# Attention and MoE kernel: the rest of q and k loaded two tokens to a partition, even tokens ahead of odd ones, and turned by halves of the partitions

## The chip, the cores and the metric

The kernel runs on one core of a Trainium2 chip. The metric is the device time of one execution in microseconds (us), where lower is better. Fast executions of one kernel agree within 1.5%. Medians below are of all executions, and ratios of the fast ones alone.

A core has five engines with queues of their own: TensorE (matmuls, "PE" in the profile, with "PEld" for its weight loads), VectorE ("DVE"), ScalarE ("ACT"), GpSimd ("POOL") and SyncE ("SP"). SyncE computes nothing here: it issues DMAs, which 16 DMA engines then carry out.

## The reference

```python
# q, k, v: (8, 8, 576, 64) float32, f: (8, 8, 576); w_in (512, 2048), w_out (2048, 512)
scores = q @ k^T / 8
cum = cumsum(log(clip(f, 1e-4, 1)), axis=-1)
scores = where(causal, scores + cum[..., :, None] - cum[..., None, :], -1e9)
attn = softmax(scores) @ v                      # "forgetting" attention
x = attn.transpose(0, 2, 1, 3).reshape(4608, 512)
h = x @ w_in
out = (h * sigmoid(h)) @ w_out
```

## The kernel before

A sequence of 576 tokens is handled as a first block of 128, then a **rest** of three blocks of 128 and a tail of 64. A **unit** is one batch and a pair of heads; there are 32. For each unit the rest of q and k passes through four steps. SyncE loads it in float32, GpSimd casts it to bf16, SyncE issues a DMA transpose (a **turn**) that puts the head dimension on the partitions, and TensorE computes scores. Between these, TensorE works off matmuls of the MoE part, the **filler work**, in an order fixed at build time.

```python
    def load_qk(n):                                   # 4 DMAs a unit, runs of 256 bytes
        b, p = divmod(n, NP)
        ts = []
        for name, src in (("qf", q), ("kf", k)):
            t = stage.tile([P, NR, 2, D], FP32, name=name, tag=name, bufs=4)
            for i in range(2):
                nc.sync.dma_start(
                    out=t[:, :, i, :],
                    in_=src[b, head(p, i), P:SM, :].rearrange("(c p) d -> p c d", p=P),
                )
            ts.append(t)
        qst[n] = tuple(ts)
    ...
    def transposes(n):                                # one turn a unit
        src = qbf.pop(n)
        t = qktp.tile([P, NX, P], BF16, name="qkT", tag="qkT")
        qkT[n] = t[:, :, :].rearrange("p x c -> p (x c)")
        nc.sync.dma_start_transpose(
            out=t[:, :, :], in_=src[:, :, :].rearrange("p x c -> p (x c)")
        )
    ...
    def prepare(n):                                   # loads run 4 units ahead, turns 2
        ...
        if n > 1 and n + 4 < NU:
            load_qk(n + 4)
        if 0 < n < NU - 2:
            cast_qk(n + 2)
            transposes(n + 2)
```

SyncE also loads v (four DMAs a batch) and the tails, and from the fifth pair of units on it turns the attention output x. All of that stands in one queue, in order.

The softmax here doesn't subtract the row's maximum and nothing guards it: scores larger than these inputs give would overflow.

## Time and profile before

| | before |
|---|---|
| time, median of 4 | 349.33 us (347.66 to 349.63) |
| profiled span, mean granted TensorE clock | 346.0 us, 0.995 |
| TensorE busy | 332.3 us (96%) |
| SyncE, from the gate behind the weights to the end of the last turn | 222.4 us: 228 issues of 199.9 us in sum, gaps 22.5 us |
| score matmuls of units 16 to 28 | one unit every 7.17 us |

The gate is a small DMA at 36 us that makes SyncE wait for half of w_out. An issue is the time that SyncE spends on one DMA instruction, not the transfer.

### The profile page before, as it was taken

Reading aid. Unit: us, or ns where it says so; the run is one execution under the profiler, and the core shown is the slowest. Engines: PE = TensorE matmul, PEld = TensorE weight load, DVE = VectorE, ACT = ScalarE, POOL = GpSimd, SP = SyncE. Lnnn points to the kernel's source line nnn. Section 1 sums busy time; section 2 is a strip of 40 time slices with the busy share of each in tenths; the row PEclk is TensorE's granted clock in tenths of the full one; section 3 lists DMA queues with packets and bytes.
Section 4 is the critical chain, followed back from the end, with each engine's and each line's share of the span. In section 5 each row is a group of like instructions: output and inputs, shape, how many; then the busy total and the mean of one; then the engine's idle time right before and its main releaser. Section 6 shows DMA issues by size and latency. Waiting matters only on the chain.

```text
span 346.0 us, 8849 instructions
## 1 busy us (share of the span) xinstructions
PE 332.3 (96%) x3521; PEld 199.3 (58%) x3567; DVE 180.2 (52%) x389; ACT 216.7 (63%) x401; POOL 128.5 (37%) x227
## 2 busy tenths in 40 slices
PE   7899999998899999999999999999999999999995
PEld 3645656576466566566565666656656565555654
DVE  4655835457267566445545545555655454344330
ACT  5757735777657857758658686585776844454431
POOL 8886316732637082163155028208320000001011
PEclk9989999999999999999999999999999999999999
DMA  8999999999999999997697979989733010001012
GB/s 153 177 189 220 184 182 163 241 211 200 174 189 214 192 197 159 167 223 164 137 213 139 170 168 184 172 171 208 139 83 66 11 61 34 30 31 63 30 50 73
DMA packets 141497, 50.44 MB, mean 146 GB/s; under 512 B 132368, under 2 KB 138768, under 8 KB 141456
## 3 DMA queue, kind: packets, MB, share of 16 engines
q1 hardware_dynamic: 131440, 32.70, 54.7%
q0 software_dynamic: 9856, 17.04, 21.7%
q8 instruction: 28, 0.46, 0.6%
q10 hardware_dynamic: 160, 0.13, 0.2%
q14 instruction: 13, 0.11, 0.1%
HBM read 36.85 MB, written 9.44 MB: 134 GB/s over the span
## 4 chain that ended last, share of the span: by engine, by line
PE 73%; DMA 16%; POOL 4%; issue 3%; SPq 3%; ACT 0%; POOLq 0%
PE po L612 31%; PE hp L567 28%; PE sc L459 6%; DMA vf<-in_v_dram 5%; PE dn L506 4%; DMA w_out_bf<-in_moe_w_out_dram 3%; DMA qktf<-in_k_dram 3%; PE dn L515 2%; DMA w_in_bf<-in_moe_w_in_dram 2%; DMA qkT<-qkb 2%; SPq L158 2%; DMA qkb<-in_k_dram 1%; POOL vp L413 1%; DMA kf<-in_k_dram 1%; SPq L168 1%
## 5 line engine op out<-in xcount | busy, mean ns | idle before, releaser
L576 DVE SCALAR_TENSOR_TENSOR gt<-th,hp 128x384 bf16<-128x384 bf16 (+2 forms) x208 | 105.5, 521 | 84.7 <-ACT th L575 81.3
L575 ACT ACTIVATE th<-hp 128x384 bf16<-128x384 f32 (+2 forms) x208 | 95.2, 479 | 86.3 <-PE hp L567 84.2
L612 PE MATMUL po<-w_out_bf,gt 128*128 128x512 bf16 (+1 forms) x551 | 139.1, 374 | 3.5 <-issue 2.1
L567 PE MATMUL hp<-x,w_in_bf 128*128 128x384 bf16 (+2 forms) x700 | 129.5, 323 | 1.2 <-DVE xt L554 0.7
L567 PEld LDWEIGHTS <-w_in_bf 128*128 128x128 bf16 x832 | 80.1, 98 | 57.6 <-issue 2.6
L591 POOL DMA_DIRECT2D out_dram<-osb x38 | 20.9, 553 | 169.9 <-ACT osb L622 122.6
L463 ACT ACTIVATE u<-sc 128x1024 bf16<-128x1024 f32 (+1 forms) x96 | 75.2, 822 | 10.9 <-PE sc L459 10.9
L612 PEld LDWEIGHTS <-gt 128*128 128x128 bf16 x592 | 53.2, 98 | 48.6 <-issue 3.2
L413 POOL TENSOR_TENSOR vp<-vf,w_bf 128x520 bf16<-128x520 f32 (+1 forms) x32 | 34.5, 1083 | 14.9 <-DMA vf<-in_v_dram 9.4
L622 ACT ACTIVATE osb<-po 128x512 f32<-128x512 f32 (+1 forms) x37 | 22.1, 596 | 18.9 <-PE po L612 18.9
L468 DVE TENSOR_TENSOR u<-u,tri 128x768 bf16<-128x768 bf16 x32 | 22.1, 689 | 21.8 <-ACT u L463 21.8
L459 PE MATMUL sc<-qkT 64*128 64x128 bf16 (+1 forms) x640 | 26.7, 207 | 1.7 <-DMA qkT<-qkb 1.6
L459 PEld LDWEIGHTS <-qkT 64*128 64x128 bf16 x640 | 18.3, 94 | 13.1 <-issue 9.5
L482 DVE TENSOR_TENSOR ut<-ut,trit 128x128 bf16<-128x128 bf16 x32 | 8.2, 257 | 32.6 <-ACT ut L475 32.6
L475 ACT ACTIVATE ut<-sc 128x640 bf16<-128x640 f32 x32 | 23.3, 729 | 0.0
L399 POOL CAST qkb<-qf 128x384 bf16<-128x384 f32 x32 | 16.7, 523 | 16.2 <-PE tp L285 11.8
L506 PEld LDWEIGHTS <-u 128*128 128x128 bf16 x576 | 20.8, 97 | 2.5
L506 PE MATMUL dn<-vp,u 128*128 128x65 bf16 x384 | 21.8, 193 | 0.0
L524 DVE TENSOR_TENSOR xr<-dn,rec 128x448 bf16<-128x448 f32 x32 | 20.0, 624 | 1.1
L506 PE MATMUL dn<-v,u 128*128 128x65 bf16 x192 | 19.8, 193 | 0.0
L567 PE MATMUL hp<-xt,w_in_bf 128*128 128x256 bf16 x128 | 17.7, 273 | 0.0
L399 POOL CAST qkb<-kf 128x384 bf16<-128x384 f32 x32 | 16.9, 527 | 1.0 <-DMA kf<-in_k_dram 1.0
(68 smaller groups left out, 203.9 us busy)
## 6 DMA issues: line engine op xcount, KB each, us to landing
out_dram<-osb POOLq DMA_DIRECT2D x32, 256.0 KB, 3.1
vf<-in_v_dram SPq DMA_DIRECT2D x26, 256.0 KB, 4.7
qf<-in_q_dram SPq DMA_DIRECT2D x64, 96.0 KB, 3.4
kf<-in_k_dram SPq DMA_DIRECT2D x64, 96.0 KB, 3.3
w_in_bf<-in_moe_w_in_dram POOLq DMA_DIRECT2D x4, 512.0 KB, 7.6
w_out_bf<-in_moe_w_out_dram POOLq DMA_DIRECT2D x4, 512.0 KB, 8.7
vf<-in_v_dram POOLq DMA_DIRECT2D x6, 256.0 KB, 9.8
qkb<-in_q_dram POOLq DMA_DIRECT2D x8, 128.0 KB, 5.4
```

Of the source, the lines that this page charges most:

```text
L399: nc.gpsimd.tensor_copy(out=t2[:, c0 : c0 + NR, :].rearrange("p c x -> p (c x)"), in_=t[:, :, :, :].rearrange("p c h d -> p (c h d)"),)
L413: nc.gpsimd.tensor_tensor(out=vbf[b][r, c, :, :], in0=vst[b][c][r, :, :], in1=w_bf[r, c + 1, b * H : (b + 1) * H, None].to_broadcast([n, H ...
L459: nc.tensor.matmul(sc[:, i, o : o + q1 - q0], lhsT=kt, rhs=t[r, q0:q1], start=True, stop=True)
L463: nc.scalar.activation(out=u[:, :, c * SM : c * SM + w], in_=sc[:, :, 0:w], func=ACT.Exp, scale=scale)
L468: nc.vector.tensor_tensor(out=x, in0=x, in1=tri[:, None, None, :].to_broadcast([P, 2, NR, P]), op=ALU.mult,)
L475: nc.scalar.activation(out=ut[:, :, 0:3:2, :].rearrange("p k i t -> p i k t"), in_=sc[:, :, T0 : T0 + (NM + 1) * ST].rearrange("p i (k t) ...
L506: nc.tensor.matmul(dn[:, i * NR + c - 1, :], lhsT=u[:, i, o : o + P], rhs=vals(kb, i), start=(kb == 0), stop=(kb == c),)
L567: nc.tensor.matmul(hp[:, :], lhsT=w_in_bf[:, cc, fc * P : (fc + 1) * P], rhs=xcols(g, cc), start=(cc == 0), stop=(cc == NCC - 1),)
L575: nc.scalar.activation(out=th[:, :], in_=hp[:, :], func=ACT.Tanh, scale=0.5)
L576: nc.vector.scalar_tensor_tensor(out=gt[:, fc, :], in0=th[:, :], scalar=1.0, in1=hp[:, :], op0=ALU.add, op1=ALU.mult,)
L612: nc.tensor.matmul(po[:, :], lhsT=gt[:, fc, tb * P : (tb + 1) * P], rhs=w_out_bf[:, fc, m0:m1], start=(fc == 0), stop=(fc == NFC - 1),)
L622: nc.scalar.activation(out=osb[:, :], in_=po[:, :], func=ACT.Copy, scale=0.5)
```

## The change

The intent is to lighten the DMA engines. Two neighbouring tokens of one head are 512 contiguous bytes in HBM (the chip's main memory), so a partition that takes both gets one run of 512 bytes in place of two of 256. A block of 128 tokens then fills 64 partitions. The two halves of the partitions hold different blocks, so each half is turned by itself. Tokens of a block now stand even ones first, and v, the masks, the decay weights and the output rows follow that order.

```diff
     def load_qk(n):
-        for name, src in (("qf", q), ("kf", k)):
-            t = stage.tile([P, NR, 2, D], FP32, name=name, tag=name, bufs=4)
-            for i in range(2):
+        t = stage.tile([P, NR, 2, 2 * D], FP32, name="qkf", tag="qkf", bufs=4)
+        for j in range(NR):
+            for half in range(2):
+                i, c = HALVES[half][j]
                 nc.sync.dma_start(
-                    out=t[:, :, i, :],
-                    in_=src[b, head(p, i), P:SM, :].rearrange("(c p) d -> p c d", p=P),
+                    out=t[half * HP : (half + 1) * HP, j, :, :],
+                    in_=(q, k)[i][b, h0 : h0 + 3 : 2, P + c * P : 2 * P + c * P, :].rearrange(
+                        "h (p s) d -> p h (s d)", s=2
+                    ),
                 )
...
     def load_v(b, c):
+            for s in range(2):
+                nc.sync.dma_start(
+                    out=t[s * HP : (s + 1) * HP, :, 0:D],
+                    in_=src.rearrange("h (p s) d -> s p h d", s=2)[s],
+                )
...
     def transposes(n):
-        nc.sync.dma_start_transpose(
-            out=t[:, :, :], in_=src[:, :, :].rearrange("p x c -> p (x c)")
-        )
+        for i in range(2):
+            half = 1 - i
+            nc.sync.dma_start_transpose(
+                out=t[:, i, :].rearrange("p (x c) -> p x c", c=HP),
+                in_=src[half * HP : (half + 1) * HP, :, :].rearrange("p x c -> p (x c)"),
+            )
...
-        fill(0.2, 1, (1, 0))
         if m > 0:
             back(m - 1)
...
-        slot(piece - 0.2)
+        slot(piece, 1, 0)
```

Cut from the diff are the table `HALVES` (which block goes to which half), `h0`, the old lines of `load_v` and its tail case, the casts, the new mask, the reordered exponentials of the decay, the column offsets of the score matmuls, and the output rows stored in two parts.

More of the change, by code (lines that the diff above doesn't have):

```diff
@@ L49 @@
     NRUN = P // RUN
+    HP = P // 2
     assert D == 64 and S == 576 and DM == H * D and NP == NCC and B == 8
@@ L78 @@
     trit = const.tile([P, ST], BF16, name="trit")
+    tri2 = const.tile([P, P], BF16, name="tri2")
     ban = const.tile([P, NP, P], BF16, name="ban")
@@ L114, in rows_of @@
         if g < 3:
-            b = tb if g == 0 else 4 + 2 * (g - 1) + tb
-            return [(slice(0, P), b, 0)]
+            t0 = (tb if g == 0 else 4 + 2 * (g - 1) + tb) * S
+            return [(slice(0, P), out[t0 : t0 + P, :])]
         for b in range(B):
             if REST_OF[b] == g:
-                return [(slice(0, P), b, P + tb * P)]
+                t0 = b * S + P + tb * P
+                rows = out[t0 : t0 + P, :].rearrange("(p s) m -> s p m", s=2)
+                return [(slice(s * HP, (s + 1) * HP), rows[s]) for s in range(2)]
         b0 = (0 if g == 3 + NM else NM) + 2 * tb
-        return [(slice(0, ST), b0, SM), (slice(ST, P), b0 + 1, SM)]
+        t0s = [(b0 + i) * S + SM for i in range(2)]
+        return [(slice(i * ST, (i + 1) * ST), out[t0 : t0 + ST, :]) for i, t0 in enumerate(t0s)]
     qk0: dict[int, bass.AP] = {}
@@ L141, in load_v0 @@
         vf0[b] = t
-    qst: dict[int, tuple] = {}
+    qst: dict[int, bass.AP] = {}
     tst: dict[int, bass.AP] = {}
@@ L150, in head @@
         return p // 2 * 4 + 2 * i + p % 2
+    HALVES = ([(0, 0), (0, 2), (1, 0)], [(1, 1), (1, 2), (0, 1)])
     def load_qk(n):
         b, p = divmod(n, NP)
-        ts = []
-        for name, src in (("qf", q), ("kf", k)):
-            t = stage.tile([P, NR, 2, D], FP32, name=name, tag=name, bufs=4)
-            for i in range(2):
+        t = stage.tile([P, NR, 2, 2 * D], FP32, name="qkf", tag="qkf", bufs=4)
+        h0 = head(p, 0)
+        for j in range(NR):
+            for half in range(2):
+                i, c = HALVES[half][j]
                 nc.sync.dma_start(
-                    out=t[:, :, i, :],
-                    in_=src[b, head(p, i), P:SM, :].rearrange("(c p) d -> p c d", p=P),
-                )
-            ts.append(t)
-        qst[n] = tuple(ts)
+                    out=t[half * HP : (half + 1) * HP, j, :, :],
+                    in_=(q, k)[i][b, h0 : h0 + 3 : 2, P + c * P : 2 * P + c * P, :].rearrange(
+                        "h (p s) d -> p h (s d)", s=2
+                    ),
+                )
+        qst[n] = t
     def load_tails(b):
@@ L177, in load_v @@
         t = vfs[c]
-        r = slice(0, P) if c < NR else slice(ST, P)
-        nc.sync.dma_start(
-            out=t[r, :, 0:D],
-            in_=v[b, :, P + c * P : min(S, P + (c + 1) * P), :].rearrange("h p d -> p h d"),
-        )
+        src = v[b, :, P + c * P : min(S, P + (c + 1) * P), :]
+        if c < NR:
+            for s in range(2):
[3 more added lines that the diff above has]
+                )
+        else:
+            nc.sync.dma_start(out=t[ST:P, :, 0:D], in_=src.rearrange("h p d -> p h d"))
         vst[b].append(t)
@@ L253, in weights_scan @@
         nc.vector.tensor_scalar_mul(out=half[:, :], in0=cum[:, S - 1 : S], scalar1=0.5)
-        nc.scalar.activation(
-            out=wexp[:, 0:S], in_=cum[:, :], func=ACT.Exp, bias=half[:, 0:1], scale=-1.0
-        )
+        for r in (slice(0, P), slice(SM, S)):
+            nc.scalar.activation(
+                out=wexp[:, r], in_=cum[:, r], func=ACT.Exp, bias=half[:, 0:1], scale=-1.0
+            )
         nc.vector.tensor_scalar(
@@ L264, in weights_scan, with weights_rest @@
         )
+    def weights_rest():
+        nc.scalar.activation(
+            out=wexp[:, P:SM].rearrange("b (c s p) -> b c p s", s=2, p=HP),
+            in_=cum[:, P:SM].rearrange("b (c p s) -> b c p s", s=2, p=HP),
+            func=ACT.Exp,
+            bias=half[:, 0:1],
+            scale=-1.0,
+        )
+        nc.vector.tensor_copy(out=wexp[:, S : S + ST], in_=wexp[:, SM:S])
     def weights():
@@ L396, in cast_qk @@
         t2 = conv.tile([P, NX, 2 * D], BF16, name="qkb", tag="qkb")
-        for i, t in enumerate(qst.pop(n)):
-            c0 = i * (NR + 1)
-            nc.gpsimd.tensor_copy(
-                out=t2[:, c0 : c0 + NR, :].rearrange("p c x -> p (c x)"),
-                in_=t[:, :, :, :].rearrange("p c h d -> p (c h d)"),
-            )
+        t = qst.pop(n)
+        for x0, j0, j1 in ((0, 0, 2), (5, 2, 3)):
+            for j in range(j0, j1):
+                nc.gpsimd.tensor_copy(
+                    out=t2[:, x0 + 2 * j - 2 * j0 : x0 + 2 * j - 2 * j0 + 2, :].rearrange(
+                        "p s (h d) -> p s h d", h=2
+                    ),
+                    in_=t[:, j, :, :].rearrange("p h (s d) -> p s h d", s=2),
+                )
         nc.gpsimd.tensor_copy(
-            out=t2[:, NR, :].rearrange("s (i d) -> s i d", i=2),
+            out=t2[:, 4, :].rearrange("s (i d) -> s i d", i=2),
             in_=tst[b].rearrange("s (u i w) d -> s u w i d", u=2, w=2)[:, p // 2, p % 2, :, :],
@@ L424, in transposes @@
         src = qbf.pop(n)
-        t = qktp.tile([P, NX, P], BF16, name="qkT", tag="qkT")
-        qkT[n] = t[:, :, :].rearrange("p x c -> p (x c)")
-        nc.sync.dma_start_transpose(
-            out=t[:, :, :], in_=src[:, :, :].rearrange("p x c -> p (x c)")
-        )
+        t = qktp.tile([P, 2, NX * HP], BF16, name="qkT", tag="qkT")
+        qkT[n] = t[:, :, :].rearrange("p i c -> p (i c)")
+        for i in range(2):
[3 more added lines that the diff above has]
+                in_=src[half * HP : (half + 1) * HP, :, :].rearrange("p x c -> p (x c)"),
+            )
+    Q0 = NX * HP
+    QAT = {1: Q0, 2: Q0 - P, 3: Q0 + P, NM: Q0 + 2 * P}
+    KAT = {1: Q0 + 2 * P + HP, 2: 0, 3: P, NM: P + HP}
     T0 = P
     CHUNKS = [
-        [(1, 0, P, 0), (2, P, 2 * P, P), (3, 2 * P, RB, 2 * P), (1, P, 2 * P, RB)],
-        [(0, 0, RB, 0), (1, 2 * P, RB, RB)],
-        [(2, 2 * P, RB, 0)] + [(kb, RB, RQ, T0 + kb * ST) for kb in range(NM + 1)],
+        [(1, QAT[1], P, 0), (2, QAT[2], P, P), (3, QAT[3], P, 2 * P), (1, QAT[2], P, RB)],
+        [(0, QAT[2], RB, 0), (1, QAT[3], P, RB)],
+        [(2, QAT[3], P, 0)] + [(kb, QAT[NM], ST, T0 + kb * ST) for kb in range(NM + 1)],
     ]
@@ L440 @@
     AT = {(c, c): (c - 1) * P for c in range(1, NM)}
-    AT |= {(c, 0): SM + (c - 1) * P for c in range(1, NM)}
+    AT |= {(2, 0): SM, (1, 0): SM + P, (3, 0): SM + 2 * P}
     AT |= {(2, 1): RB, (3, 1): SM + RB, (3, 2): 2 * SM}
@@ L450, in scores @@
         sc = psc.tile([P, 2, SM], FP32, name="sc", tag="sc")
-        for kb, q0, q1, o in CHUNKS[c]:
+        for kb, q0, nq, o in CHUNKS[c]:
             for i in range(2):
                 r = slice(i * D, (i + 1) * D)
-                if kb == 0:
-                    kt = kT0[b][r, p, :]
-                else:
-                    k0 = RB if kb == NM else kb * P + RB
-                    kt = t[r, k0 : k0 + P]
+                kt = kT0[b][r, p, :] if kb == 0 else t[r, KAT[kb] : KAT[kb] + P]
                 nc.tensor.matmul(
-                    sc[:, i, o : o + q1 - q0], lhsT=kt, rhs=t[r, q0:q1], start=True, stop=True
+                    sc[:, i, o : o + nq], lhsT=kt, rhs=t[r, q0 : q0 + nq], start=True, stop=True
                 )
@@ L470, in scores @@
                 in0=x,
-                in1=tri[:, None, None, :].to_broadcast([P, 2, NR, P]),
+                in1=tri2[:, None, None, :].to_broadcast([P, 2, NR, P]),
                 op=ALU.mult,
@@ L589, in store @@
         n = max(n, 0)
-        for q_, dst, src in stores[:n]:
+        for q_, dst, src in sum(stores[:n], []):
             q_.dma_start(out=dst, in_=src)
@@ L622, in m2_part @@
             nc.scalar.activation(out=osb[:, :], in_=po[:, :], func=ACT.Copy, scale=0.5)
-            for n, (r, b, s0) in enumerate(rows_of(g, tb)):
-                t0 = b * S + s0
+            parts = []
+            for n, (r, rows) in enumerate(rows_of(g, tb)):
                 q_ = nc.gpsimd if not last else (nc.scalar if n == 1 else nc.sync)
-                stores.append((q_, out[t0 : t0 + r.stop - r.start, m0:m1], osb[r, :]))
+                parts.append((q_, rows[:, m0:m1], osb[r, :]))
+            stores.append(parts)
     M1 = [(g, fc) for g in range(NG) for fc in range(NFC)]
@@ L729 @@
     turn0(0, 1)
-    nc.vector.tensor_copy(out=wexp[:, S : S + ST], in_=wexp[:, SM:S])
+    weights_rest()
     bans = [ban0(0), ban0(1)]
@@ L782 @@
     load_v0(7)
+    for i in range(2):
+        for j in range(2):
+            make_upper_triangular(
+                nc, tri2[i * HP : (i + 1) * HP, j * HP : (j + 1) * HP], val=1.0, diag=(i <= j)
+            )
     after(w_out_bf[0:1, 2 * NFC // WQ - 1, DM - 16 : DM])
```

## The prediction

> **What bounds the kernel now.** I read the page first (engine shares, DMA queues), then busy time by stretches, the chain of waits in order of time, and last SyncE's own timeline, because the change touches little but what SyncE issues.
>
> ```profile
> PE 332.3 (96%) x3521; PEld 199.3 (58%) x3567; DVE 180.2 (52%) x389; ACT 216.7 (63%) x401; POOL 128.5 (37%) x227
> ...
> DMA  8999999999999999997697979989733010001012
> ...
> q1 hardware_dynamic: 131440, 32.70, 54.7%
> ```
> TensorE is busy for 96% of 346.0 us. The 16 DMA engines are also near full, but only to slice 28 or so (242 us). Queue q1 is SyncE's: 131440 packets of mostly 256 B.
>
> ```profile
> 40.00:90.00 50.00, 46.58 (x563) 30.35 (x569) 27.20 (x62) 31.43 (x63) 23.41 (x38) 1.00 1.07 197
> 90.00:120.00 30.00, 29.68 (x352) 17.83 (x355) 17.40 (x38) 21.33 (x39) 12.24 (x21) 1.00 1.06 193
> 120.00:240.00 120.00, 118.69 (x1378) 71.97 (x1393) 65.12 (x144) 82.18 (x154) 47.83 (x85) 1.00 0.96 177
> 280.00:346.00 66.00, 61.91 (x364) 35.67 (x368) 23.93 (x48) 26.70 (x57) 5.93 (x11) 1.00 0.13 45
> ```
> By stretches (length, TensorE busy, ..., granted clock, DMA share, GB/s): DMA runs at 1.0 from 40 to 240 us, yet TensorE idles only 3.4 us in 40 to 90 and 1.6 us in the next 150. The chain tells the same:
>
> ```profile
> 85.24 3.53 DMA qkT<-qkb
> 88.82 0.40 PE sc L459 x8
> 89.21 0.97 PE po L612 x4
> 90.18 0.44 PE hp L567 x4
> ```
> Up to 88.8 us the chain that ended last runs through loads and turns (DMA transposes) of q and k; after it, through TensorE alone. Four 512-column matmuls take 0.86 to 0.97 us there, some 0.22 to 0.24 us each, and a TensorE that waits for nothing can't be sped up by lighter DMA. All that a perfect load path could win is the idle 3.4 us of 40 to 90: 1% of the span.
>
> The resource that I think decides the case is SyncE's queue:
>
> ```profile
> 129.50 1.10 SPq L158 DMA_DIRECT2D qf<-in_q_dram  x2
> 130.65 1.02 SPq L158 DMA_DIRECT2D kf<-in_k_dram  x2
> 131.78 1.23 SPq L427 DMA_TRANSPOSE qkT<-qkb  x1
> 133.05 2.12 SPq L158 DMA_DIRECT2D qf<-in_q_dram  x2
> 135.22 1.02 SPq L158 DMA_DIRECT2D kf<-in_k_dram  x2
> 136.35 1.22 SPq L427 DMA_TRANSPOSE qkT<-qkb  x1
> 137.61 0.63 SPq L168 DMA_DIRECT2D qktf<-in_q_dram  x1
> 138.28 0.63 SPq L168 DMA_DIRECT2D qktf<-in_k_dram  x1
> 139.01 1.27 SPq L538 DMA_TRANSPOSE x<-xr  x1
> 140.33 1.23 SPq L542 DMA_TRANSPOSE xt<-xr  x1
> ```
> It issues one DMA after another with gaps of some 0.05 us. Summed from this timeline, its issues fill 203 of the 225 us between 37 and 262 us (90%).
>
> ```profile
> L427 SPq DMA_TRANSPOSE qkT<-qkb x32: 1220/1370/2697, 53.4 to 257.9; - x32
> L158 SPq DMA_DIRECT2D kf<-in_k_dram x64: 486/487/1766, 38.0 to 246.0; - x64
> L179 SPq DMA_DIRECT2D vf<-in_v_dram x32: 521/627/2807, 54.9 to 233.9; - x32
> L538 SPq DMA_TRANSPOSE x<-xr x11: 1212/1235/2253, 126.9 to 266.0; - x11
> ```
> These are least, median and longest ns of one issue. The least does not follow the bytes: a turn of seven 128x128 blocks and one of six cost 1.22 and 1.21 us (the one-block xt turn 1.22), and a load some 0.5 us whatever its size.
>
> **What the Trainium skill says.** "Perfetto Trace Analysis", section "DMA Instruction — HWDGE": the profiled window of such an instruction is the locking and use of the descriptor generator, not data movement. Its section "What 'DMA-bound' means" lists, beside the DMA engines, the DMA sequencer, seen as solid DMA slices on the issuing engine's track. The trace agrees: SyncE is 90% solid. "DMA: Bandwidth & Descriptors", section "Specifications", puts the least transfer for line rate at 512 B. In the packet records a 256 B packet takes 18 ns (median; mean 23 under load) and a 4096 B one some 160, so the time does not scale down with size: this is what the change goes for. The same page, "Rules for kernel authors", advises against two transfers to disjoint partition halves in place of one of 128 partitions, since they serialize; the change makes such halves of q/k, v and the turns. No transfer before the change is such a pair, so the trace can't say yet.
>
> **The change part by part.** "Unit" is a head pair of a batch; there are 32, at some 7.1 us of TensorE each in the steady part (score matmuls begin every 14.2 us per pair of units; about 5 us a unit before 90 us).
>
> *Packets, removed.* A unit's q/k rest is 1536 packets of 256 B, then 768 of 512 B. Going by 18 ns and 160 ns, a 512 B packet should take 18 + 256 x 142/3840 = 27 to 28 ns (estimate), so a pair saves 36 - 27.5 = 8.5 ns. These packets are 38% of a unit's 4032 (1536 q/k, 896 v, 256 tails, 896 turn, 448 x turns), so DMA load falls by about a tenth, 0.96 to 0.87. Worth nothing after 90 us, as TensorE does not wait; up to some 2 us of the 3.4 us before.
>
> *SyncE issues, added.* Loads: 4 to 6 a unit, 192 for 128, so +64 at 0.55 us with the gap = +35 us. v: three of four tiles loaded in halves, +24 at 0.67 us (64-partition issues took 0.62 us) = +16 us. Turns: 64 half turns for 32 whole ones. If the 1.22 us is per instruction, +32 x 1.27 = +41 us. If it goes by partitions, 0.61 each, +0. A mixture of base and size, 0.87 each, gives +15 us. Sum: +51, +66 or +92 us.
>
> *SyncE time that can take it.* 22 us of gaps, plus the part of today's issues above their floors. Floors are 127 x 0.49 + 32 x 1.23 + 32 x 0.58 + 20 x 1.23 + 16 x 0.62 = 155 us of the 203, so 48 us is pushback from full DMA engines. It should mostly go with smaller, lighter transfers, but not all, as the weights still stream at 40 us. So 50 to 70 us is free against 51 to 92 us added.
>
> *By the unit.* New floor in the stretch with x turns: loads 6 x 0.56 = 3.35, v 1.75 x 0.67 = 1.17, tails 0.34, x turns 1.27, together 6.1 us, plus half turns 1.3 to 2.55: **7.4 to 8.7 us against 7.1 us of TensorE.** A whole turn now lands some 11 us before its scores (issued at 111.6 and landing in about 4, for scores at 126.7), so a deficit shows only once it has eaten that: at 1.6 us a unit over 20 units, 32 - 11 = 21 us, plus some 5 us early, where TensorE is at 5 us a unit; at 0.75 us, 15 - 11 = 4 us; at 0.35 us, nothing.
>
> *TensorE.* The build has the same 7127 rows on it; only four blocks of four matmuls change places, around the first turns of x. 0.3 us either way. ScalarE gets two more small exponentials at the start, about 0.6 us in the shadow of the v load. VectorE's masks keep their shape. GpSimd: three casts of 256 columns for two of 384, at 0.5 us each for 384 now, roughly +0.2 us a unit; 24 more store issues at 0.55 us = 13 us; masks 1.6 us. It is busy 37%. Hidden.
>
> **The rivals.** (1) *Hidden anyway*: DMA engines relax, SyncE just copes, TensorE stays the bound, and one wait near 88 us shortens: 346 to 350 us. For it: TensorE at 96%, the one stretch of idling, the slack of 11 us; and the moved filler looks like a retuning of something that worked. (2) *SyncE becomes the bound*: waits for DMA qkT in front of the scores, in the steady part. For it: 90% solid, 51 to 92 us of added issues, and floors of a turn that did not fall from seven blocks to one. Against: all turns seen have 128 partitions, so how the issue goes with partitions is unseen. Time: 353 us with the mixture, 370 to 376 with full price. (3) *DMA was secretly the bound and all speeds up by 2% or more*: would need TensorE waits that aren't there. Below 342.6 us, unlikely. (4) *Half transfers are slow on the DMA engines themselves* (landing later than 3.8 us a turn): adds a few us to (2), and the build's eight completion semaphores, each reused after eight issues, would then hold SyncE too.
>
> **Range and chances.** I weigh rival 1 at 0.45 (348), the mixture at 0.27 (353), full price at 0.28 (370). The middle of that is about 351 us. Low end: 349.6 less the whole early idling and some spread, 344.5. High end: full price, 374. Faster by over 2% (below 342.6) needs rival 3: 0.05. Within 2%: 0.60. Slower by over 2% (above 356.6): 0.35.
>
> **What would show it.** Right: fewer packets on q1 (by 24,576), DMA share of 120 to 240 us below 0.9; load issues at 0.5 to 0.6 us; TensorE idle of 40 to 90 us not above 3.4 us in rival 1, against SyncE above 95% solid and TensorE waits on DMA qkT after 100 us in rival 2. The least issue time of the half turn decides between them: 0.6, 0.9 or 1.2 us. Wrong: if TensorE stalls come with SyncE idle (then landing or GpSimd is it), if the time falls under 342 us (then DMA load slowed TensorE unseen), or if pushback stays at 48 us though packets fell.

## The result

The changed kernel took **431.02 us** in the median (430.27 to 431.91, 4 runs). Its results are right. The ratio to the kernel before is 1.235 (95% interval 1.230 to 1.240): a fourth slower, and far above the predicted range. Ratios here are the mean time of one kernel's runs over that of the other's in the same rounds, so they are not quite the ratio of the medians quoted. Executions over 1.5% slower than the fastest of the same kernel are left out of the means.

First the page of the changed kernel (shares of busy time, DMA busy in 40 slices, SyncE's queue):

```profile
PE 359.1 (84%) x3567; PEld 206.9 (48%) x3567; DVE 181.2 (42%) x389; ACT 223.0 (52%) x403; POOL 145.1 (34%) x291
...
DMA  9999757546465565456555646574566431112123
...
q1 hardware_dynamic: 109296, 32.71, 35.7%
```

The packets did get fewer: 22,144 less on q1, and the DMA engines are half idle. Still the time rose by 82 us. Busy time by stretches, with the columns as before:

```profile
40.00:90.00 50.00, 43.26 (x496) 26.92 (x493) 21.71 (x49) 25.91 (x49) 18.19 (x34) 0.93 0.66 144
90.00:120.00 30.00, 19.47 (x196) 11.44 (x196) 9.56 (x22) 11.87 (x21) 9.31 (x18) 0.83 0.55 128
120.00:240.00 120.00, 96.02 (x996) 52.84 (x994) 48.37 (x104) 63.30 (x111) 37.45 (x77) 0.91 0.57 126
```

The DMA share of the last stretch is 0.57 for 0.96, but most of that fall is only the slower kernel, which moves 126 GB/s for 177. The packets of all queues sum to 240 us per DMA engine over the whole span, for 268 before: a tenth less. TensorE, which idled 1.3 us there, now idles 24 us, and its granted clock is 0.91 for 1.00. What it waits for is told by the waits of TensorE (who waited for what: us in total, times, longest). First before, then after:

```profile
PE sc L459 <- DMA qkT<-qkb: 1.6, 1, 1.6
```

```profile
PE sc L492 <- DMA qkT<-qkb: 58.4, 17, 6.9
```

The scores wait for turns. The chain that ended last says who holds the turns back; first before, then after:

```profile
PE 73%; DMA 16%; POOL 4%; issue 3%; SPq 3%; ACT 0%; POOLq 0%
```

```profile
PE 39%; SPq 26%; DMA 10%; issue 5%; POOL 4%; ACT 1%; DVE 1%; POOLq 0%
```

"SPq" is SyncE's sequencer at work on issues: 3% of the span before, 26% after. Here is one unit of its timeline in the changed kernel (start, length, what, how many):

```profile
144.12 2.52 SPq L459 DMA_TRANSPOSE qkT<-qkb  x2
146.68 0.60 SPq L180 DMA_DIRECT2D qktf<-in_q_dram  x1
147.33 0.63 SPq L180 DMA_DIRECT2D qktf<-in_k_dram  x1
148.01 0.64 SPq L169 DMA_DIRECT2D qkf<-in_q_dram  x1
148.69 1.49 SPq L169 DMA_DIRECT2D qkf<-in_k_dram  x1
150.22 0.61 SPq L169 DMA_DIRECT2D qkf<-in_q_dram  x1
150.87 1.25 SPq L169 DMA_DIRECT2D qkf<-in_k_dram  x2
152.17 0.60 SPq L169 DMA_DIRECT2D qkf<-in_q_dram  x1
152.88 2.52 SPq L459 DMA_TRANSPOSE qkT<-qkb  x2
```

From turn to turn are 8.76 us, without v and without turns of x. Least, median and longest ns of one issue:

```profile
L459 SPq DMA_TRANSPOSE qkT<-qkb x64: 1198/1263/2473, 54.4 to 344.2; - x64
L169 SPq DMA_DIRECT2D qkf<-in_q_dram x96: 596/606/1432, 36.2 to 334.3; - x96
```

A half turn costs what a whole one did, and a load of 64 KB costs more than one of 96 KB did. SyncE's stretch from the gate to the last turn grew from 222.4 to 309.2 us, that is by 86.8 us; the profiled span grew by 84.0. By the records, TensorE idles 57 us more in it, and is busy 27 us longer with the same work at a lower granted clock (0.932 for 0.995).

### The profile page after: what moved, and what is told of

The parts are those of the page before. It is cut to its first block, busy times and chain, and to the rows that moved or that the text cites. A ratio compares the mean times of both kernels' runs of the same rounds, so it can differ in the third digit from the quotient of the medians.

```text
span 430.0 us, 9108 instructions
## 1 busy us (share of the span) xinstructions
PE 359.1 (84%) x3567; PEld 206.9 (48%) x3567; DVE 181.2 (42%) x389; ACT 223.0 (52%) x403; POOL 145.1 (34%) x291
## 4 chain that ended last, share of the span: by engine, by line
PE 39%; SPq 26%; DMA 10%; issue 5%; POOL 4%; ACT 1%; DVE 1%; POOLq 0%
PE po L645 17%; PE hp L600 16%; SPq L169 10%; SPq L459 8%; DMA vf<-in_v_dram 4%; DMA qkT<-qkb 4%; SPq L193 3%; PE sc L492 3%; SPq L575 2%; POOL vp L443 2%; PE dn L539 2%; POOL qkb L427 2%; DMA x<-xr 1%; SPq L571 1%; PE dn L548 1%
## 5 line engine op out<-in xcount | busy, mean ns | idle before, releaser
L645 PE MATMUL po<-w_out_bf,gt 128*128 128x512 bf16 (+1 forms) x592 | 155.5, 394 | 0.0
L600 PE MATMUL hp<-x,w_in_bf 128*128 128x384 bf16 (+2 forms) x704 | 136.2, 335 | 4.4 <-DMA x<-xr 4.2
L600 PEld LDWEIGHTS <-w_in_bf 128*128 128x128 bf16 x832 | 83.6, 102 | 67.1 <-issue 13.8
L645 PEld LDWEIGHTS <-gt 128*128 128x128 bf16 x592 | 55.4, 101 | 53.6 <-issue 12.3
L492 PE MATMUL sc<-qkT 64*128 64x128 bf16 (+1 forms) x640 | 30.2, 216 | 60.9 <-DMA qkT<-qkb 58.4
L624 POOL DMA_DIRECT2D out_dram<-osb x62 | 33.1, 538 | 124.9 <-ACT osb L655 98.3
L427 POOL CAST qkb<-qkf 128x256 bf16<-128x256 f32 x96 | 37.5, 418 | 69.6 <-DMA qkf<-in_k_dram 46.4
L492 PEld LDWEIGHTS <-qkT 64*128 64x128 bf16 x640 | 19.9, 98 | 74.5 <-DMA qkT<-qkb 65.5
L501 DVE TENSOR_TENSOR u<-u,tri 128x768 bf16<-128x768 bf16 x32 | 19.0, 592 | 76.0 <-ACT u L496 76.0
L492 PE MATMUL sc<-qkT,kT 64*128 64x64 bf16 (+1 forms) x128 | 16.4, 265 | 0.0
## 6 DMA issues: line engine op xcount, KB each, us to landing
vf<-in_v_dram SPq DMA_DIRECT2D x56, 128.0 KB, 3.5
out_dram<-osb POOLq DMA_DIRECT2D x54, 128.0 KB, 2.7
```

Of the source, the lines that this page charges most:

```text
L427: nc.gpsimd.tensor_copy(out=t2[:, x0 + 2 * j - 2 * j0 : x0 + 2 * j - 2 * j0 + 2, :].rearrange("p s (h d) -> p s h d", h=2), in_=t[:, j, :, ...
L492: nc.tensor.matmul(sc[:, i, o : o + nq], lhsT=kt, rhs=t[r, q0 : q0 + nq], start=True, stop=True)
L600: nc.tensor.matmul(hp[:, :], lhsT=w_in_bf[:, cc, fc * P : (fc + 1) * P], rhs=xcols(g, cc), start=(cc == 0), stop=(cc == NCC - 1),)
L624: q_.dma_start(out=dst, in_=src)
L645: nc.tensor.matmul(po[:, :], lhsT=gt[:, fc, tb * P : (tb + 1) * P], rhs=w_out_bf[:, fc, m0:m1], start=(fc == 0), stop=(fc == NFC - 1),)
```

## The experiments

Theory A says that SyncE's issue time is the bound of the changed kernel. Its rivals: B, the half-partition transfers are slow in the DMA engines; C, the new layout or the moved filler work costs on the computing engines; and, later, D, half turns cost something beyond their issue. All versions gave right results. In every round the kernel before ran on the same chip, with medians of 345.67 to 348.32 us.

### Issues without data: `b_tiny`

```diff
 # kernel before, in load_qk, twice a unit
+            for _ in range(2):
+                nc.sync.dma_start(out=tiny[...][:, :], in_=ident_bf[0:1, 0:16])
```

> The kernel before plus 128 DMAs of 32 bytes (on-chip to on-chip) in SyncE's queue, four for each head pair's loads: nearly as many extra issues as the change has (120), no halves, no extra data. Theory A (SyncE's issue time is the bound of the changed kernel): each issue adds about 0.6 us plus a 0.045 us gap, 2.6 us a head pair, 83 us in all, of which gaps and pushback of the kernel before can absorb 20 to 40 us: 390 to 415 us, SyncE over 90% solid and waits of TensorE on DMA qkT of tens of us. Theory B (the half-partition transfers themselves are slow in the DMA engines): at most 355 us. Theory C (the changed layout on TensorE, GpSimd casts or the moved filler work is what costs): 347 to 353 us.

Measured: **414.07 us**, ratio 1.190 (1.185 to 1.196). The waits of TensorE and SyncE's tiny issues:

```profile
PE sc L465 <- DMA qkT<-qkb: 36.0, 15, 5.9
```

```profile
L167 SPq DMA_DIRECT2D tiny<-ident_bf x128: 502/584/1747, 38.2 to 315.7; - x128
```

DMAs of 32 bytes, with the kernel before otherwise untouched, reproduce four fifths of the loss. An issue of 32 bytes takes 0.58 us, and 128 of them cost 66 us. The DMA share of 120 to 240 us falls to 0.72 here too, with every packet of before still moved. B and C are out as the main cause.

### Halves of the loads, and of the turns: `b_qkhalf`, `b_turn2`

```diff
 # b_qkhalf: kernel before
+                for r in (slice(0, P // 2), slice(P // 2, P)):
+                    nc.sync.dma_start(out=t[r, :, i, :], in_=rows[r, :, :])
 # b_turn2: kernel before
+        for r in (slice(0, P // 2), slice(P // 2, P)):
+            nc.sync.dma_start_transpose(
+                out=t[:, :, r], in_=src[r, :, :].rearrange("p x c -> p (x c)")
+            )
```

> The kernel before with each rest load of q and k cut in two by partitions (0 to 63, 64 to 127): 8 issues a head pair for 4, the same 256-byte packets and bytes, results right. Theory A: the same +128 issues as with the tiny ones, so within 10 us of that run, 390 to 415 us. Theory B: markedly slower than the tiny ones, by 15 us or more, since the halves themselves would cost. Theory C: 347 to 353 us.

> The kernel before with each turn of q and k made in two halves of the partitions, as the change does, and nothing else: +32 transposes, results right. Theory A: a half turn costs the full 1.2 us of SyncE, so +41 us of issues, 1.27 us a head pair: SyncE floor 7.1 to 7.5 us a head pair against 7.1 of TensorE in the steady part, and about 8 against 5 to 6 early: 358 to 375 us. If pushback is absorbed entirely: 350 to 355 us. Theory B: the same or more than A, with landing times of a turn above 3.8 us. Theory C: 347 to 353 us.

Measured: `b_qkhalf` **425.13 us** (1.220, 1.214 to 1.225), `b_turn2` **369.64 us** (1.063, 1.058 to 1.067). The halved loads come out 11 us above the tiny ones, between what A and B expected. Their issues explain it: SyncE's sum is 275.5 us for 261.9, since a 64-partition load takes 0.61 us in the median where a whole one takes 0.49 (k) or 0.58 (q) in the kernel before. The halved turns are where A put them, with the full price a half:

```profile
L428 SPq DMA_TRANSPOSE qkT<-qkb x64: 1193/1263/2462, 52.6 to 281.8; - x64
```

### Issues taken away from the changed kernel: `a_load4`, `a_vpool`, `a_load4_vpool`

```diff
 # a_load4: q in partitions 0 to 63, k in 64 to 127, three blocks in one DMA
+        for half, src in enumerate((q, k)):
+            for i in range(2):
                 nc.sync.dma_start(
+                    out=t[half * HP : (half + 1) * HP, :, i, :],
+                    in_=src[b, head(p, i), P:SM, :].rearrange("(c p s) d -> p c (s d)", s=2, p=HP),
                 )
 # a_vpool: rest loads of v
-                nc.sync.dma_start(
+                nc.gpsimd.dma_start(
```

Not shown: in `a_load4` the casts, the columns of the scores and the order of the two half turns follow the new places.

> The changed kernel with q in partitions 0 to 63 and k in 64 to 127, so that all three blocks of one head and tensor come in one DMA: 4 loads a head pair for 6, the same 512-byte packets, bytes and half turns, results right. Theory A: -64 issues of 0.65 us, 42 us off SyncE, and while SyncE is the bound the time falls by as much: 387 to 400 us. Theory B (halves slow in the DMA engines): the same bytes to the same partitions, so 425 to 435 us. Theory C: 425 to 435 us.

> The changed kernel with the 56 rest loads of v issued from GpSimd's queue in place of SyncE's: same bytes, halves and packets. Theory A: 56 x 0.68 = 38 us off SyncE, so 390 to 402 us, unless GpSimd (34% busy, +56 issues of 0.6 to 0.9 us, in order with stores that wait for ScalarE) becomes a wait of its own. Theory B and C: 425 us or more, since the transfers and the compute are the same.

> Both reliefs in one: the changed kernel with 4 loads of q and k a head pair and v from GpSimd, 120 issues off SyncE, which leaves about as many as the kernel before has, still with 32 more turns. SyncE floor a head pair 2.6 + 0.3 + 1.3 + 2.6 = 6.8 us against 7.1 of TensorE. Theory A: TensorE is the bound again, 347 to 360 us. Theory B or C: 420 us or more. If it comes out under 346 us the lighter packets are worth something after all.

Measured: `a_load4` **391.68 us** (1.123, 1.117 to 1.130), `a_vpool` **394.69 us** (1.134, 1.126 to 1.142), both together **366.42 us** (1.054, 1.048 to 1.061). The same bytes, data packets and half turns in 64 issues fewer are 39 us faster, 0.61 us an issue. B and C expected nothing of either. The two together missed A's 347 to 360 us by 6 us; what is left is close to what half turns alone cost in `b_turn2`.

The account over the runs so far, from SyncE's timelines (stretch from the gate to the end of the last turn):

| kernel | issues | their sum, us | stretch, us | time less stretch, us |
|---|---|---|---|---|
| before | 228 | 199.9 | 222.4 | 126.9 |
| `b_turn2` | 260 | 231.0 | 246.3 | 123.3 |
| `a_load4_vpool` | 228 | 225.5 | 246.4 | 120.0 |
| `a_load4` | 284 | 252.3 | 271.4 | 120.3 |
| `a_vpool` | 292 | 253.7 | 274.6 | 120.1 |
| `b_tiny` | 356 | 261.9 | 286.1 | 128.0 |
| `b_qkhalf` | 356 | 275.5 | 300.3 | 124.8 |
| after | 348 | 285.5 | 309.2 | 121.8 |

Over a spread of 82 us in time, the time less SyncE's stretch stays within 120 to 128 us. By itself this doesn't show who holds up whom: in `a_load4_kact` below the difference is 125.5 us as well, though SyncE issues for only 208.5 of its 277.3 us there. What points to SyncE is that its issues fill the stretch. After the change they take 285.5 of 309.2 us, and 347 gaps of 0.044 us (median) some 15 more, which leaves about 8 us for real waits.

### Controls: `b_vpool`, `a_load4_kact`, `a_load4_kact_vpool`, `b_kact`, `a_load4_kact_fill`

```diff
 # b_vpool: kernel before, rest loads of v on nc.gpsimd
 # ..._kact: the two k loads of a unit
-                nc.sync.dma_start(
+                (nc.sync, nc.scalar)[half].dma_start(
 # ..._fill: fill(0.2, 1, (1, 0)) and slot(piece - 0.2) put back as in the kernel before
```

> Control: the kernel before with its 32 rest loads of v issued from GpSimd, 32 issues (about 29 us) off SyncE. Theory A, with TensorE as the bound of the kernel before: 345 to 351 us, no gain over 1%. If SyncE bounded the kernel before as well, it should fall by 10 us or more.

> The changed kernel with 4 loads a head pair, of which the two of k are issued from ScalarE's queue: 64 more issues of 0.68 us (44 us) off SyncE, on ScalarE instead (56% busy, +0.6 us each, 38 us). SyncE's issues then sum to some 208 us, about the 200 of the kernel before. Theory A (SyncE's issue time is the whole cost): TensorE is the bound again, 346 to 354 us, with waits of TensorE on DMA qkT of under 5 us. Rival: half turns cost beyond their issues (landing, DMA engines): 360 us or more, as in the version with v on GpSimd. Another way to miss: ScalarE's in-order queue makes exponentials late, seen as TensorE idle that no DMA ends.

> The same, with v from GpSimd as well: SyncE down to some 170 us of issues, far below TensorE's pace. Theory A: SyncE no longer matters at all, 346 to 355 us; the lighter packets of q and k then show what they are worth alone: under 344 us if DMA load slowed TensorE unseen, 346 to 350 if they were hidden anyway. v on GpSimd cost the kernel before about 4 us, and may here.

> Control: the kernel before with its k loads from ScalarE's queue, 64 issues (39 us) off SyncE. Theory A, TensorE the bound: 345 to 351 us. It is also the rival version for the best time: if it is under 345 us, SyncE held the kernel before too.

> As the first of these, with the filler work put back where the kernel before has it (some matmuls ahead of the turns of x). The prediction held that the move is worth 0.3 us either way: within 1.5 us of the first.

Measured: `b_vpool` 351.83 us (1.012), `a_load4_kact` 402.82 us (1.155), `a_load4_kact_vpool` 423.59 us (1.225), `b_kact` 359.78 us (1.037), `a_load4_kact_fill` 403.01 us (1.163). The first says that the kernel before gains nothing from 32 issues fewer on SyncE. The last says that the moved filler work is worth nothing visible there, in a version that stalls elsewhere. The three others, all with k on ScalarE, missed what theory A expected; the expectation of `a_load4_kact` had named late exponentials as a way to miss. Its waits name the reason:

```profile
ACT th L599 <- DMA qktf<-in_k_dram: 36.4, 1, 36.4
```

The program hands out eight completion semaphores in turn over SyncE's and ScalarE's DMAs alike, and each new DMA first waits for the one that had its semaphore before. ScalarE came to its k loads at 18 us, stood from 22 us on behind DMAs that SyncE issued only from its gate on (37 us here), and held up the exponentials: 34 us of idle TensorE in one piece. So these four say nothing on half turns.

### ScalarE from unit 6 on: `b_klate`, `b_turn2_klate`, `a_load4_klate`, `a_load4_klate_vpool`

```diff
-                (nc.sync, nc.scalar)[half].dma_start(
+                (nc.scalar if half == 1 and n >= 6 else nc.sync).dma_start(
```

> The kernel before with the k loads of units 6 and later issued from ScalarE. The version with all k loads there lost 10 us in one stall near 22 us, as ScalarE's queue stood behind loads that SyncE had not issued yet; from unit 6 on that can't happen. Expected 346 to 352 us: the base line for the next run.

> The same plus half turns: SyncE's issues sum to about 231 - 31 = 200 us, as in the kernel before. Theory A (a half turn costs nothing but SyncE's issue time): within 6 us of the run without half turns, 348 to 357 us. Rival D (half turns cost beyond their issues: landing, DMA engines): 15 us or more above it, 363 us or more, as without the relief.

> The changed kernel with 4 loads, and k of units 6 and later from ScalarE: SyncE's issues about 252 - 37 = 215 us, v still on SyncE. Theory A: 350 to 362 us, as the early units still go through SyncE at over TensorE's pace. Rival D: 366 us or more.

> The same with v on GpSimd: SyncE's issues about 190 us, less than in the kernel before. Theory A: 347 to 356 us (v on GpSimd cost the kernel before 4 us). Rival D: 364 us or more. Under 343 us only if lighter packets help TensorE after all.

Measured: 351.13 us (1.013), 370.31 us (1.068), 378.00 us (1.091) and 393.84 us (1.136). Rival D seemed confirmed, but the trace doesn't bear it out. In `b_turn2_klate` the turns after unit 5 landed 7.7 to 16.4 us ahead of their scores, so they were not late. ScalarE was, behind loads again, and TensorE waited for its evictions:

```profile
ACT osb L623 <- DMA qf<-in_q_dram: 13.3, 3, 7.3
PE hp L568 <- ACT osb L623: 7.6, 4, 3.1
```

ScalarE is no place for these loads while it shares semaphores with a SyncE that waits for GpSimd. The other two were not taken apart. The test was spoilt once more, so the next one used GpSimd, whose DMAs have semaphores of their own.

### GpSimd: `b_turn2_vpool`, `a_load4_vkpool`

```diff
 # b_turn2_vpool: b_turn2 and b_vpool together
 # a_load4_vkpool: a_load4_vpool, and
-                nc.sync.dma_start(
+                (nc.gpsimd if half == 1 and n >= 6 else nc.sync).dma_start(
```

> The kernel before with half turns, and its rest loads of v from GpSimd, whose DMAs share no completion semaphores with SyncE's: SyncE's issues 231 - 29 = 202 us, as in the kernel before. To be held against the same without half turns (351.8 us). Theory A (half turns cost only issue time): 350 to 358 us. Rival D (half turns cost beyond it): 366 us or more.

> The changed kernel with 4 loads, v and the k loads from unit 6 on from GpSimd: SyncE's issues 225 - 37 = 188 us, below the kernel before's 200, and ScalarE's queue untouched. Theory A: 350 to 358 us, unless GpSimd's order (loads behind stores that wait for ScalarE) delays loads, seen as waits of its casts on DMA qkf. Rival D: 364 us or more. Under 344 us only if lighter packets help TensorE.

Measured: **365.45 us** (1.052, 1.043 to 1.061) and **361.16 us** (1.041, 1.036 to 1.047). By their times, neither fits A. In `b_turn2_vpool` the relief did not arrive: SyncE's issues between 120 and 240 us still filled 94% of the time, for the mean issue of a half turn rose to 1.52 us (1.37 in `b_turn2`). In `a_load4_vkpool` it did arrive: 79%. There the stretch of 120 to 240 us has hardly any loss left, half turns and all. Busy time by stretches, before and then this version:

```profile
62.00:120.00 58.00, 54.63 (x706) 34.77 (x713) 34.01 (x77) 42.29 (x78) 27.16 (x46) 1.00 1.07 202
```

```profile
62.00:120.00 58.00, 49.52 (x609) 30.79 (x608) 29.54 (x65) 35.64 (x66) 44.72 (x77) 0.91 1.02 176
120.00:240.00 120.00, 117.86 (x1355) 69.87 (x1353) 65.96 (x142) 81.88 (x151) 95.63 (x176) 1.00 0.96 171
```

From 120 to 240 us TensorE is busy 117.86 us at full clock, against 118.69 before. A unit takes 7.22 us there (units 16 to 28), against 7.17 before, 7.70 in `b_turn2` and 10.00 in the changed kernel. That speaks against D for the steady part: with SyncE below its limit, half turns cost nothing visible. It is one version, and the DMA engines are as full there as before (0.96), so it doesn't show what lighter DMA load is worth.

Most of the 11 us of span that remain arise between 62 and 120 us: the scores of unit 10 begin 8.3 us later than before. TensorE idles 5 us more there, and runs 49.5 us of work at a clock of 0.91, which I estimate at another 4 to 5 us. GpSimd is busy 77% of that stretch, with the v and k loads added to its work, and SyncE waits for it (33 us in all on its conversions of v). Up to 75 us, where k still goes through SyncE, SyncE's issues fill 95% of the time. After that they do not bound: they fill 63% of 90 to 105 us, for 91% before. The chain that ended last runs there through GpSimd, and then through this landing (start, length, what):

```profile
100.69 9.08 DMA qkT<-qkb
```

A half turn landed 9.1 us after its issue, while GpSimd had issued seven loads of v from 96.6 to 101.3 us, and TensorE waited 4.0 us for it. Late landings are not proper to half turns. In `b_vpool`, with whole turns and v on GpSimd, 14 of 32 turns took over 6 us to land (1 of 32 in the kernel before), and TensorE waited 6.2 us for two of them. In `b_turn2` and the changed kernel, with v on SyncE, no half turn took over 6 us. So the late landings came with v on GpSimd; why they do was not tested. No version beat the kernel before.

## Why the prediction was wrong

- **What bounds the kernel before:** right. That lighter packets win nothing is not contradicted, since no version came out under the kernel before, but none had lighter packets and nothing else changed. DMA load fell by a tenth, as predicted (240 us per engine for 268); the share of 0.57 makes it look like more. A 512 B packet took 27 ns (median of the packet records), as estimated. The forecast of 24,576 packets fewer missed by 2,432, because each added DMA brings packets of its own: 16 a load in `b_qkhalf`, 32 a turn in `b_turn2`, and 88 x 16 + 32 x 32 = 2,432.
- **That SyncE decides, and the mark to know it by:** right in mechanism, given too little weight. Rival 2 is what happened: SyncE issuing back to back, and waits of TensorE on DMA qkT after 100 us. "SyncE above 95% solid" was too strict a mark. It was 94% in 120 to 240 us, and the rest is gaps between issues and short waits.
- **The half turn (0.6, 0.87 or 1.22 us):** 1.20 us at least, 1.26 in the median. The evidence shown in the prediction (one block, six and seven at the same price) already pointed to a price per instruction, yet that case got 0.28 of the weight. `b_turn2` shows it.
- **"Loads: ... +64 at 0.55 us with the gap":** mis-sized. A 64-partition load takes 0.606 us, and 0.656 in the mean, so six of them with gaps take 4.2 us a unit for the 3.35 predicted. The prediction had the 0.62 us of 64-partition issues at hand, and used it for v alone. Its sentence that no transfer before the change is a pair of halves is a misreading: the tails of q and k go to partitions 0 to 63 and 64 to 127, one after the other.
- **"So 50 to 70 us is free":** this step failed most. Least issue times summed to 151.6 us before and 258.6 after, +107.1 us, where the prediction's full price was +92 (its 203 of 225 us of SyncE before come to 199.9 of 222.4, issue by issue). What stands above them (the pushback) fell only from 48.3 to 26.8 us, and gaps rose from 22.5 to 23.7, as each of 120 more issues brings its own. So 20 us were absorbed for the 50 to 70 counted on: 107.1 - 21.5 + 1.2 = 86.8 us, the growth of the stretch.
- **"Has eaten that: ... 32 - 11 = 21 us":** the unit at full price was 10.0 us in the steady part for 8.7 predicted, so the deficit was 2.8 us a unit for 1.6. The lead of 11 us was that of unit 10 alone: in the kernel before, turns of units 10 to 29 landed 5.4 to 14.6 us ahead of their scores. In the changed kernel, 15 of units 8 to 29 began their scores within 0.1 us of the landing. Nor was the lead spent for good: the last two turns, with no loads in front of them, landed 11.0 and 8.8 us ahead. Time less stretch fell by 5 us, not by 11.
- **TensorE, ScalarE, VectorE, GpSimd hidden:** nothing speaks against it, and `b_tiny` has four fifths of the loss without any of these changes. Putting the filler work back made no difference, but only a version that stalled elsewhere was tried. A clock below 1.00 was not foreseen; it came with the stalls.
- **Rival 4, slow half transfers:** refuted as a cause. A half turn lands in 2.7 us in the median for 3.8, a load in 2.4 to 2.6 for 3.3 to 3.4. The semaphore remark in it proved right elsewhere, for ScalarE.

## What to carry to other kernels

Before splitting a DMA to please the DMA engines, count the issues of the queue that carries it. Multiply them by the issue time that the profile shows, and hold the sum against what the bounding engine takes for the same stretch. A queue that is 90% solid has only its real waits to spare. Its gaps come with every issue, and of its pushback (issue time above the least) less than half went away here, 21.5 of 48.3 us. Moving DMAs to another engine's queue helps only if that engine can afford to stand still behind them.

## What the Trainium skill lacked or had wrong

- "DMA: Bandwidth & Descriptors", section "Issuing engines are not separate DMA queues", calls the sequencer's time to initiate a DMA "usually small relative to the DMA itself". One by one that holds here (0.58 us an issue for 2.1 us to landing with 32 bytes). What that section lacks is that the issues of one queue add up: 128 such DMAs cost 66 us, and SyncE's issue time set the time of the changed kernel.
- The same page, "Rules for kernel authors", rightly advises against two transfers to disjoint partition halves, because they share the DMA engines. In these runs the cost was in the issue (`b_qkhalf` +77 us, with 0.61 us for each half), while the DMA share of 120 to 240 us fell from 0.96 to 0.68.
- No page that I found gives, in microseconds and for this chip, the issue time of a transpose from on-chip memory: at least 1.2 us, for one block of 128x128 or seven, with 128 partitions or 64. A load from SyncE takes 0.49 to 0.63 us in the median, from 32 bytes to 256 KB, and a 64-partition one no less than a whole one.
- "DMA: Bandwidth & Descriptors", section "Specifications", asks for 512 B for line rate. The runs agree on the packet (27 ns for two of 18). It won nothing here: no version with such packets came out under the kernel before, which TensorE bounds, though none had them alone.
- "Perfetto Trace Analysis", section "DMA Optimizations", suggests balancing DMAs across engines where issuing is the bottleneck. It lacks that an in-order compute queue can stall behind shared completion semaphores (34 us in one piece with k on ScalarE), and that turns can land later with loads on GpSimd, whose semaphores are its own (`b_vpool`: +4 us, 14 of 32 turns over 6 us).
